# Weight conversion in a gated recurrence with an activation layer: three VectorE operations a tile instead of six, listed beside the first two groups' chunks

## The chip, the cores and the metric

One core of one Trainium2 chip. The metric is the device time of one launch in microseconds (us); the time before is the median of three runs. The engines are named as the profile names them: PE (TensorE, with its weight loads as PEld), DVE (VectorE), ACT (ScalarE), POOL (GpSimd) and SP (SyncE, here the engine that issues nearly all transfers).

## The reference

Inputs are q, k, v, a_re and a_im of shape (4, 8, 768, 48) and two weight matrices, w_in (384 x 2048) and w_out (2048 x 384), which are float64; the output is float32, 3072 x 384.

```
mag = sqrt(a_re^2 + a_im^2);  scale = min(mag, 0.999) / (mag + 1e-6)
a = (a_re + i a_im) * scale
for t in range(768):                       # for each of 4 x 8 heads
    S = a[t][:, None] * S + outer(k[t], v[t])     # S is complex, 48 x 48
    y[t] = q[t] @ real(S)
x = y as (4*768) x (8*48)
h = x @ w_in;  g = h * cos(h);  out = g @ w_out
```

## The kernel before

The 768 steps of each of four sequences are cut into chunks of 128 steps; two chunks make a group (G = 2), so there are 24 chunks and 12 groups. The recurrence is computed in chunks: decays are turned into logarithms and phases and summed along the steps by matmuls with a triangular matrix (L666, L703); scaled and turned keys and queries are transposed; a chunk's scores and values are matmuls; a state passes from chunk to chunk.

For each group the work comes in stages, each a function:

- g_log, g_prod, g_angle (L631 to L697): logarithms, exponentials and the arctangent on ACT, with DVE and POOL operations between, in scratch tiles that exist once. g_prod also sends a row through DRAM and back by six small transfers (L679).
- gates (L840): g_phase (L699), g_trig (L712), g_stack (L720), then four f_transpose (L733; for both chunks the keys kT and the queries qT). An f_transpose is one DVE block transpose (L738) and twelve small transfers issued by SP (L747).
- chunks (L851): f_scores (L752), f_state (L782) and f_out (L763) for the two chunks, then f_xt (L801), ten transfers that assemble the columns for the layer.
- mm1 (L812), eight times a group: the first layer's matmuls for 256 columns of the hidden dimension (L817), then x cos(x) by ACT (L823, L623) and DVE (L824, L826, L828).
- mm2 (L831), twice a group: the second layer's 16 matmuls (L834), a copy out of PSUM by ACT (L837) and the output's transfer.

The main loop (L873) is a software pipeline: turn `it` does the gates of group it, the chunks of group it-1, mm1 of group it-2 and mm2 of group it-3. In a turn mm2 is listed first; the others are woven: weave (L863) gives every step of a part a place between the part's two bounds and lists all steps in the order of their places. The list is a priority and not the order itself: the framework lets each engine take the earliest listed instruction that its timing model finds ready, and fixes each engine's order so; each engine then executes its instructions strictly in that order.

The weights arrive as float64 and have to become float32. weight_parts (L564) cuts them into 28 tiles, 12 of w_in (128 x 512) and 16 of w_out (128 x 384). from_double (L578) loads a tile of 64-bit words by a transfer from SP (L586, two buffers `raw`), and works on the high and low 32-bit words, which are every second word of `raw`. DVE moves exponent and mantissa into place (L591), adds the sign (L593), adds the three top bits of the low word (L595), and takes the rounding bit (L597); POOL adds it as an integer (L599); DVE takes the exponent (L601) and sets to zero what is too small for float32 (L603). These are six DVE operations and one POOL operation a tile, with two buffers `t` for the rounding bit and the exponent.

All 28 tiles are listed in turn 0, in the last four fifths of group 0's gates (L884).

When the fast path has ended, a flag decides whether the general path has to run: the tile `least` collects whether a decay became too small; its minimum goes through DRAM onto one partition and into a register (L906 to L919).

Of the kernel before, what the change touches and what calls it, by code (L numbers as in the profile page):

```python
# [485 lines left out]
def fast_path(ctx, tc, q, k, v, a_re, a_im, moe_w_in, moe_w_out, out, least):  # L486
# [91 lines left out]
    def from_double(dst, src):  # L578

        n = dst.shape[1]
        raw = stage.tile([C, n], I64, tag="raw", name="raw")
        nc.sync.dma_start(out=raw, in_=src)  # L586
# [4 lines left out]
        nc.vector.tensor_scalar(out=bits, in0=hi, scalar1=3, scalar2=0x3FFFFFF8,  # L591
                                op0=ALU.logical_shift_left, op1=ALU.bitwise_and)
        nc.vector.scalar_tensor_tensor(out=bits, in0=hi, scalar=0xC0000000, in1=bits,  # L593
                                       op0=ALU.bitwise_and, op1=ALU.bitwise_or)
        nc.vector.scalar_tensor_tensor(out=bits, in0=lo, scalar=29, in1=bits,  # L595
                                       op0=ALU.logical_shift_right, op1=ALU.bitwise_or)
        nc.vector.tensor_scalar(out=t, in0=lo, scalar1=28, scalar2=1,  # L597
                                op0=ALU.logical_shift_right, op1=ALU.bitwise_and)
        nc.gpsimd.tensor_tensor(out=bits, in0=bits, in1=t, op=ALU.add)  # L599
        e = stage.tile([C, n], U32, tag="t", name="t")  # L600
        nc.vector.tensor_scalar(out=e, in0=hi, scalar1=20, scalar2=0x7FF,  # L601
                                op0=ALU.logical_shift_right, op1=ALU.bitwise_and)
        nc.vector.scalar_tensor_tensor(out=dst, in0=e, scalar=897.0, in1=dst,  # L603
                                       op0=ALU.is_ge, op1=ALU.mult)


# [205 lines left out]
    def mm1(g, jp):  # L812
# [10 lines left out]
        nc.scalar.activation(out=turn, in_=ps, func=AF.Identity, scale=INV_TWO_PI, bias=quarter_b)  # L823
# [7 lines left out]
    def mm2(g, i):  # L831
        ps = pm.tile([C, DM], F32, tag="m", name="op")
        for j in range(NJ):
            nc.tensor.matmul(ps, lhsT=X[g]["gate"][j // 2][:, j % 2, ts(i, C)], rhs=w_out[:, j],  # L834
                             start=(j == 0), stop=(j == NJ - 1))
# [36 lines left out]
    weights = weight_parts()  # L872
    for it in range(NG + 3):  # L873
# [22 lines left out]
def kernel(ctx, tc, q, k, v, a_re, a_im, moe_w_in, moe_w_out, out):  # L896
# [7 lines left out]
    fast_path(tc, q, k, v, a_re, a_im, moe_w_in, moe_w_out, out, least)  # L904
# [4 lines left out]
    line_d = scratch.tile([D2], F32, name="line_d")  # L909
    nc.sync.dma_start(out=line_d, in_=low.rearrange("p o -> (p o)"))  # L910
    line = keep.tile([1, D2], F32, name="line")
# [39 lines left out]
```

## Time and profile before

| | us |
|---|---|
| median of 3 runs (844.55 to 846.62) | 845.02 |
| the profiled execution, whole | 846.44 |
| its span, first to last instruction | 844.6 |
| PE busy (81% of the span) | 682.8 |
| DVE busy (62%) | 526.6 |
| PEld busy (60%) | 506.9 |
| ACT busy (40%) | 338.8 |
| POOL busy (18%) | 152.3 |

A row of a group has the line, the engine, the operation, out<-in by the names of the program, the shapes and the count, then the busy time of the group in us and the mean of one in ns, then the idle time of the engine just before these instructions and what ended it. A row of a timeline has the start and the duration in us. A row of the waits has the waiting instruction, what it waited for, the sum in us, the count and the longest. In the page's strips each of the 40 digits is the busy share of one slice in tenths.

### The profile page before, as it was taken

How to read it: one execution, taken by the hardware profiler on the slowest of the kernel's cores; microseconds unless marked ns; L12 is line 12 of the kernel's file. 1: busy time of each engine (PE TensorE's matmuls, PEld its weight loads, DVE VectorE, ACT ScalarE, POOL GpSimd, SP SyncE). 2: the span in 40 equal slices, each digit the busy share in tenths (PEclk: the TensorE clock that was granted, in tenths of full speed). 3: DMA queues.
4: the chain of work that ended last, by engine and by line, in shares of the span. 5: the costliest groups of instructions: out<-in, count | busy, mean ns of one | idle time of the engine just before them, and what ended most of it. 6: DMA issues, size and time to landing. Idle time of an engine off the chain costs nothing.

```text
span 844.6 us, 10236 instructions
## 1 busy us (share of the span) xinstructions
PE 682.8 (81%) x3464; PEld 506.9 (60%) x3464; DVE 526.6 (62%) x833; ACT 338.8 (40%) x492; POOL 152.3 (18%) x96
## 2 busy tenths in 40 slices
PE   1201043368999999999999999999999999999997
PEld 0000023256678587586785875867858758678684
DVE  3997988666468566485675764856757648335060
ACT  5313001415535645356345453563454534214140
POOL 1433433320120300301203003012030030000000
PEclk9999975579999999999999999999999999999999
DMA  8533347225243362352622623526226231210000
GB/s 181 124 118 102 99 138 167 53 60 98 51 96 73 67 127 51 62 115 51 125 49 54 119 49 62 116 51 131 45 54 117 50 70 29 51 45 15 24 0 22
DMA packets 251335, 65.66 MB, mean 78 GB/s; under 512 B 230270, under 2 KB 247678, under 8 KB 251274
## 3 DMA queue, kind: packets, MB, share of 16 engines
q1 hardware_dynamic: 250674, 64.62, 36.0%
q8 instruction: 29, 0.48, 0.2%
q10 hardware_dynamic: 600, 0.30, 0.1%
q14 instruction: 32, 0.26, 0.1%
HBM read 36.51 MB, written 4.76 MB: 49 GB/s over the span
## 4 chain that ended last, share of the span: by engine, by line
PE 56%; DVE 15%; SPq 9%; ACT 8%; POOL 6%; issue 3%; DMA 3%; DVEq 0%; POOLq 0%; ACTq 0%
PE hp L817 23%; PE op L834 18%; SPq L747 7%; PE sc L758 4%; PE sp L789 2%; POOL m L650 2%; PE yp L772 2%; POOL w_out L599 2%; PE lgs L666 2%; ACT rs L623 2%; PE phs L703 2%; PE yp L776 2%; PE phs L706 1%; DVE gate L826 1%; ACT L622 1%
## 5 line engine op out<-in xcount | busy, mean ns | idle before, releaser
L817 PE MATMUL hp<-xT,w_in 128*128 128x256 f32 x1152 | 267.5, 385 | 4.3 <-DVE gate L828 3.7
L834 PE MATMUL op<-w_out,gate 128*128 128x384 f32 x768 | 251.1, 486 | 0.0
L817 PEld LDWEIGHTS hp<-xT,w_in 128*128 128x128 f32 x1152 | 214.8, 192 | 36.8 <-DVE gate L828 4.1
L834 PEld LDWEIGHTS op<-w_out,gate 128*128 128x128 f32 x768 | 145.9, 190 | 99.2
L823 ACT ACTIVATE turn<-hp,quarter_b 128x512 f32<-128x512 f32 x96 | 65.8, 685 | 111.2 <-PE hp L817 110.0
L623 ACT ACTIVATE gate<-gate 128x512 f32<-128x512 f32 x96 | 60.1, 627 | 91.6 <-DVE gate L826 89.8
L828 DVE TENSOR_TENSOR gate<-hp,gate 128x512 f32<-128x512 f32 x96 | 65.4, 685 | 37.1 <-ACT gate L623 35.2
L824 DVE TENSOR_SCALAR gate<-turn 128x512 f32<-128x512 f32 x96 | 40.3, 420 | 75.7 <-ACT turn L823 74.5
L666 PE MATMUL lgs<-m,sums 128*128 128x384 f32 x48 | 22.8, 606 | 73.2 <-POOL m L650 73.2
L826 DVE TENSOR_TENSOR gate<-turn,gate 128x512 f32<-128x512 f32 x96 | 65.5, 685 | 1.7
L795 POOL TENSOR_TENSOR state<-state,end 96x384 f32<-96x384 f32 x16 | 16.4, 1023 | 263.1 <-DVE state L793 166.7
L758 PEld LDWEIGHTS sc<-qT,kT 96*128 96x128 f32 x384 | 51.7, 201 | 16.4 <-issue 10.4
L666 PEld LDWEIGHTS lgs<-m,sums 128*128 128x128 f32 x48 | 9.6, 222 | 84.5 <-POOL m L650 80.3
L837 ACT COPY ot<-op 128x384 f32<-128x384 f32 x24 | 11.3, 472 | 121.0 <-PE op L834 113.8
L758 PE MATMUL sc<-qT,kT 96*128 96x128 f32 x384 | 52.4, 286 | 8.2 <-DMA qT<-tr 8.2
L650 POOL TENSOR_TENSOR m<-m,rs 128x768 f32<-128x768 f32 x12 | 21.7, 1809 | 206.4 <-ACT rs L623 204.1
L703 PE MATMUL phs<-sq,sums 128*128 128x384 f32 x48 | 22.4, 556 | 43.5 <-DVE sq L694 43.5
L772 PE MATMUL yp<-atm,v 128*48 128x128 f32 x384 | 39.4, 289 | 21.2 <-DVE atm L760 21.2
L760 DVE TENSOR_TENSOR atm<-sc,causal 128x512 f32<-128x512 f32 x48 | 32.7, 682 | 20.6 <-PE sc L758 20.6
L708 DVE TENSOR_SCALAR ph<-phs 128x384 f32<-128x384 f32 x24 | 13.3, 554 | 50.4 <-PE phs L706 36.3
L772 PEld LDWEIGHTS yp<-atm,v 128*48 128x48 f32 x384 | 23.0, 128 | 30.2 <-issue 24.9
L653 DVE SCALAR_TENSOR_TENSOR sq<-mag,sq 128x768 f32<-128x768 f32 x12 | 11.5, 959 | 46.8 <-POOL mag L652 46.8
(72 smaller groups left out, 824.4 us busy)
## 6 DMA issues: line engine op xcount, KB each, us to landing
kT<-tr SPq DMA_DIRECT2D x288, 32.0 KB, 2.0
qT<-tr SPq DMA_DIRECT2D x288, 32.0 KB, 1.8
raw<-in_moe_w_in_dram SPq DMA_DIRECT2D x12, 512.0 KB, 4.0
raw<-in_moe_w_out_dram SPq DMA_DIRECT2D x16, 384.0 KB, 3.4
re<-in_a_re_dram SPq DMA_DIRECT2D x24, 192.0 KB, 3.2
im<-in_a_im_dram SPq DMA_DIRECT2D x24, 192.0 KB, 4.2
k<-in_k_dram SPq DMA_DIRECT2D x24, 192.0 KB, 3.9
q<-in_q_dram SPq DMA_DIRECT2D x24, 192.0 KB, 3.9
```

What stands on the lines that cost most here:

```text
L623: chain(nc.scalar.activation(func=func, **kw))
L666: nc.tensor.matmul(ps, lhsT=sums, rhs=x["lg"][:, ts(i, DM)], start=True, stop=True)
L703: nc.tensor.matmul(ps, lhsT=sums, rhs=x["turn"][:, ts(i, DM)], start=True, stop=first)
L747: nc.sync.dma_start(out=place[ts(b, 32), a], in_=tr[ts(a, 32), b])
L758: nc.tensor.matmul(ps[:, h], lhsT=y["kT"][:, hh * HH + h], rhs=queries(y, hh * HH + h), start=True, stop=True)
L772: nc.tensor.matmul(ps[ds(side * 64, D), p], lhsT=vals[:, 2 * p + side], rhs=y["atm"][:, 2 * p + side], start=True, stop=(state is None))
L817: nc.tensor.matmul(ps[:, ji], lhsT=w_in[:, dc, ts(jp * 2 + ji, C)], rhs=x["xT"][:, dc].rearrange("p g t -> p (g t)"), start=(dc == 0), sto ...
L823: nc.scalar.activation(out=turn, in_=ps, func=AF.Identity, scale=INV_TWO_PI, bias=quarter_b)
L824: nc.vector.tensor_scalar(out=cs, in0=turn, scalar1=ROUND, scalar2=ROUND, op0=ALU.add, op1=ALU.subtract)
L826: nc.vector.tensor_tensor(out=cs, in0=turn, in1=cs, op=ALU.subtract)
L828: nc.vector.tensor_tensor(out=gate, in0=ps, in1=cs, op=ALU.mult)
L834: nc.tensor.matmul(ps, lhsT=X[g]["gate"][j // 2][:, j % 2, ts(i, C)], rhs=w_out[:, j], start=(j == 0), stop=(j == NJ - 1))
```

## The change

from_double now has three DVE operations a tile. The high word is moved and given its sign as before. The low word goes through an ACT Identity: read as an integer, multiplied by 2^-29, plus 2^23, written as an integer; so it is rounded to the bits that float32 keeps and carries a one in the exponent. POOL adds that to the high part. A result is thereby twice the weight, which is taken back by the scale at L823 and by a multiplication in place of the copy at L837. Nothing is set to zero any more. Instead DVE takes the exponent by two shifts into a single buffer `e`, and an ACT Relu of 897 minus the exponent, written over `e`, adds up along the tile into one column of a new tile `odd`; any value above zero sets the flag for the general path. This check needs a reduction, a comparison and one more small transfer at the end.

The 12 tiles of w_in are now listed in turn 1, over the whole turn beside the gates of group 1 and the chunks of group 0, and the 16 tiles of w_out in turn 2, beside the gates of group 2, the chunks of group 1 and mm1 of group 0. Turn 0 has no weights and is woven like all others.

```diff
-        t = stage.tile([C, n], U32, tag="t", name="t")
+        low = stage.tile([C, n], U32, tag="low", name="low")
+        e = stage.tile([C, n], U32, tag="e", name="e", bufs=1)
         bits = dst.bitcast(U32)
         nc.vector.tensor_scalar(out=bits, in0=hi, scalar1=3, scalar2=0x3FFFFFF8,
                                 op0=ALU.logical_shift_left, op1=ALU.bitwise_and)
         nc.vector.scalar_tensor_tensor(out=bits, in0=hi, scalar=0xC0000000, in1=bits,
                                        op0=ALU.bitwise_and, op1=ALU.bitwise_or)
-        nc.vector.scalar_tensor_tensor(out=bits, in0=lo, scalar=29, in1=bits,
-                                       op0=ALU.logical_shift_right, op1=ALU.bitwise_or)
-        nc.vector.tensor_scalar(out=t, in0=lo, scalar1=28, scalar2=1,
-                                op0=ALU.logical_shift_right, op1=ALU.bitwise_and)
-        nc.gpsimd.tensor_tensor(out=bits, in0=bits, in1=t, op=ALU.add)
-        e = stage.tile([C, n], U32, tag="t", name="t")
-        nc.vector.tensor_scalar(out=e, in0=hi, scalar1=20, scalar2=0x7FF,
-                                op0=ALU.logical_shift_right, op1=ALU.bitwise_and)
-        nc.vector.scalar_tensor_tensor(out=dst, in0=e, scalar=897.0, in1=dst,
-                                       op0=ALU.is_ge, op1=ALU.mult)
+        nc.scalar.activation(out=low, in_=lo, func=AF.Identity, scale=2.0 ** -29, bias=carrier_b)
+        nc.gpsimd.tensor_tensor(out=bits, in0=bits, in1=low, op=ALU.add)
+        nc.vector.tensor_scalar(out=e, in0=hi, scalar1=1, scalar2=21,
+                                op0=ALU.logical_shift_left, op1=ALU.logical_shift_right)
+        nc.scalar.activation(out=e.bitcast(F32), in_=e, func=AF.Relu, scale=-1.0, bias=least_e_b,
+                             accum_out=odd[:, ds(next(odds), 1)])
...
-        nc.scalar.activation(out=turn, in_=ps, func=AF.Identity, scale=INV_TWO_PI, bias=quarter_b)
+        nc.scalar.activation(out=turn, in_=ps, func=AF.Identity, scale=INV_TWO_PI / in_scale,
+                             bias=quarter_b)
...
-        nc.scalar.copy(out=ot, in_=ps)
+        nc.scalar.mul(out=ot, in_=ps, mul=1.0 / (in_scale * out_scale))
...
-    weights = weight_parts()
+    parts = weight_parts()
+    weights = {1: parts[:-NJ], 2: parts[-NJ:]}
...
-        if it == 0:
-            weave((gates(0), 0.0, 1.0), (weights, 0.2, 1.0))
-            continue
         if 0 <= o < NG:
             for i in range(G):
                 mm2(o, i)
         weave((gates(g) if g < NG else (), 0.0, 0.5),
               (chunks(c) if 0 <= c < NG else (), 0.0, 1.0),
+              (weights.get(it, ()), 0.0, 1.0),
...
+    even = keep.tile([C, 1], F32, name="even")
+    nc.vector.tensor_reduce(out=even, in_=odd, axis=AX.X, op=ALU.max)
+    nc.vector.tensor_scalar(out=even, in0=even, scalar1=0.0, scalar2=None, op0=ALU.is_le)
...
+    line_d = scratch.tile([D2 + C], F32, name="line_d")
+    nc.sync.dma_start(out=line_d[0:D2], in_=low.rearrange("p o -> (p o)"))
+    nc.sync.dma_start(out=line_d[D2:D2 + C], in_=even.rearrange("p o -> (p o)"))
```

More of the change, by code (lines that the diff above doesn't have):

```diff
@@ L485, in fast_path @@
 @with_exitstack
-def fast_path(ctx, tc, q, k, v, a_re, a_im, moe_w_in, moe_w_out, out, least):
+def fast_path(ctx, tc, q, k, v, a_re, a_im, moe_w_in, moe_w_out, out, least, odd):
     nc = tc.nc
@@ L903 @@
     least = keep.tile([D2, 2 * H], F32, name="least")
[L904 removed]
+    C = 128
+    odd = keep.tile([C, moe_w_in.shape[0] // C * 4 + moe_w_out.shape[0] // C], F32, name="odd")
+    fast_path(tc, q, k, v, a_re, a_im, moe_w_in, moe_w_out, out, least, odd)
     low = keep.tile([D2, 1], F32, name="low")
     nc.vector.tensor_reduce(out=low, in_=least, axis=AX.X, op=ALU.min)
+    even = keep.tile([C, 1], F32, name="even")
+    nc.vector.tensor_reduce(out=even, in_=odd, axis=AX.X, op=ALU.max)
+    nc.vector.tensor_scalar(out=even, in0=even, scalar1=0.0, scalar2=None, op0=ALU.is_le)
     scratch = ctx.enter_context(tc.tile_pool(name="scratch", bufs=1,
                                              space=bass.MemoryType.DRAM))
[L909 to L911 removed]
+    line_d = scratch.tile([D2 + C], F32, name="line_d")
+    nc.sync.dma_start(out=line_d[0:D2], in_=low.rearrange("p o -> (p o)"))
+    nc.sync.dma_start(out=line_d[D2:D2 + C], in_=even.rearrange("p o -> (p o)"))
+    line = keep.tile([1, D2 + C], F32, name="line")
     nc.sync.dma_start(out=line, in_=line_d.unsqueeze(0))
```

6 lines of the change are left out of this document (added).

## The prediction

> **What bounds the kernel now.** I read the page first, for the span and for where TensorE is idle, then the stretches, cut at the point that matters, then the groups by shape, and last the timelines of single engines. The page shows two different kernels in one span:
>
> ```profile
> span 844.6 us, 10236 instructions
> ...
> PE   1201043368999999999999999999999999999997
> ...
> DVE  3997988666468566485675764856757648335060
> ACT  5313001415535645356345453563454534214140
> ...
> PEclk9999975579999999999999999999999999999999
> ```
>
> A slice is 21.1 us. From the tenth or eleventh slice on TensorE is full and nothing else is. In the first ten it is mostly idle, and VectorE is the engine with nines. So the time is a lead-in plus a full-TensorE stretch, and the border I choose is the first matmul of the second layer for group 0 (L834), which needs nearly everything that the lead-in makes: the converted weights, two groups of attention, and the first layer of group 0.
>
> ```profile
> 188.97 1.56 PE L817 MATMUL hp<-xT,w_in 128*128 128x256 f32 x6
> ...
> 219.15 8.55 PE L834 MATMUL op<-w_out,gate 128*128 128x384 f32 x26
> ```
>
> The stretches cut there (columns: TensorE, its weight loads, VectorE, ScalarE and GpSimd busy, each with its instructions, then granted clock, DMA share, GB/s):
>
> ```profile
> 0.00:20.00 20.00, 2.92 (x4) 1.17 (x4) 5.32 (x12) 11.18 (x15) 3.77 (x6) 1.00 0.81 184
> 20.00:160.00 140.00, 28.39 (x130) 19.39 (x130) 119.88 (x219) 26.39 (x34) 51.90 (x35) 0.84 0.47 119
> 160.00:219.15 59.15, 42.95 (x236) 34.03 (x237) 35.02 (x52) 22.79 (x34) 9.30 (x6) 0.77 0.37 71
> 219.15:844.60 625.45, 608.53 (x3095) 452.31 (x3093) 366.39 (x553) 278.42 (x411) 87.37 (x49) 1.00 0.33 66
> ```
>
> Behind 219.15 TensorE is busy 608.53 of 625.45 us (97%). Before it, TensorE is busy 74.3 of 219.15 us, and VectorE 119.88 of the 140 us from 20 to 160 (86%). Each us by which L834 starts earlier is a us off the end, as long as the 625.45 us behind it stay as they are. Call the start of L834 T; now T = 219.15.
>
> **VectorE's part of the conversion.** These are all of its groups, 28 tiles, 12 of w_in and 16 of w_out:
>
> ```profile
> L593 DVE SCALAR_TENSOR_TENSOR w_out<-raw,w_out 128x384 uint32<-128x384 uint32 x16 | 10.4, 652 | 0.0
> L595 DVE SCALAR_TENSOR_TENSOR w_in<-raw,w_in 128x512 uint32<-128x512 uint32 x12 | 9.8, 815 | 0.0
> L603 DVE SCALAR_TENSOR_TENSOR w_out<-t,w_out 128x384 f32<-128x384 uint32 x16 | 8.9, 558 | 9.9 <-POOL w_out L599 9.9
> L595 DVE SCALAR_TENSOR_TENSOR w_out<-raw,w_out 128x384 uint32<-128x384 uint32 x16 | 8.8, 551 | 0.0
> L591 DVE TENSOR_SCALAR w_in<-raw 128x512 uint32<-128x512 uint32 x12 | 8.2, 686 | 0.0
> L603 DVE SCALAR_TENSOR_TENSOR w_in<-t,w_in 128x512 f32<-128x512 uint32 x12 | 8.2, 683 | 2.8 <-POOL w_in L599 2.8
> L593 DVE SCALAR_TENSOR_TENSOR w_in<-raw,w_in 128x512 uint32<-128x512 uint32 x12 | 8.2, 681 | 0.0
> L591 DVE TENSOR_SCALAR w_out<-raw 128x384 uint32<-128x384 uint32 x16 | 6.7, 420 | 0.0
> L601 DVE TENSOR_SCALAR t<-raw 128x384 uint32<-128x384 uint32 x16 | 5.7, 353 | 0.0
> L597 DVE TENSOR_SCALAR t<-raw 128x384 uint32<-128x384 uint32 x16 | 5.6, 353 | 0.0
> L601 DVE TENSOR_SCALAR t<-raw 128x512 uint32<-128x512 uint32 x12 | 5.0, 417 | 0.0
> L597 DVE TENSOR_SCALAR t<-raw 128x512 uint32<-128x512 uint32 x12 | 5.0, 416 | 0.0
> ```
>
> Out go L595 (9.8 + 8.8), L597 (5.0 + 5.6) and L603 (8.2 + 8.9): 46.3 us. What stays is L591 (14.9), L593 (18.6) and a TENSOR_SCALAR of L601's shape with two shifts in place of a shift and a mask (10.7): 44.2 us. With L603 goes its wait for GpSimd's sum, 9.9 + 2.8 us on VectorE. VectorE's work ahead of T falls from 5.32 + 119.88 + 35.02 = 160.2 us to 113.9, of which 5.3 lie in the first 20 us, which are spent on the loads and group 0's first chain and do not change. That leaves 108.6 us behind 20.
>
> How fast it can be packed is what I have to choose. From 20 to 160 the profile has it at 0.856, from 20 to 219.15 at 154.9 / 199.15 = 0.778. At the first T = 20 + 108.6 / 0.856 = 147, at the second 20 + 108.6 / 0.778 = 160. With no gap at all it would be 129. The weights' new place in the lists speaks for the better half: their work can now lie beside the chunks and the first layer of group 0, where VectorE has gaps today (35.02 of 59.15 us), and no longer has to be over before group 1's gates. I take the middle, T = 153: 66 us earlier.
>
> **What ScalarE takes over.** Two activations a tile, 56 in all: an Identity with a bias column, and a Relu with a bias column and an accumulator. No row shows them on integers, on every second word, or with an accumulator. The nearest rows:
>
> ```profile
> L623 ACT ACTIVATE gate<-gate 128x512 f32<-128x512 f32 x96 | 60.1, 627 | 91.6 <-DVE gate L826 89.8 <-DVE flag L916 1.8
> ...
> L622 ACT ACT_TABLE_LOAD x24 | 30.8, 1283 | 3.0 <-issue 2.6
> ...
> L691 ACT ACTIVATE rs<-sq,half_b 128x768 f32<-128x768 f32 x12 | 11.2, 936 | 0.4 <-ACT sq L623 0.2
> ...
> L623 ACT ACTIVATE mag<-m 128x768 f32<-128x768 f32 x12 | 10.1, 840 | 19.7 <-DVE qs L728 19.4
> ```
>
> Without a bias column 256 elements more cost 840 - 627 = 213 ns, 0.83 ns each, so an Identity with a column is 936 - 213 = 723 ns at 512 and 936 - 320 = 616 ns at 384. Both activations: 12 x 1.446 + 16 x 1.232 = 37 us. Bounds: without the column's price 12 x 2 x 0.627 + 16 x 2 x 0.520 = 32 us; with every one at the 768-wide 0.936, which leaves 0.2 to 0.3 us for an accumulator, 52 us. ScalarE is busy 11.18 + 26.39 + 22.79 = 60.4 us ahead of T now, so 97 (92 to 113). In 153 us that is 64%. I cost it at nothing on the path; the cover is ScalarE's idle time, and what it costs when that is too small is the first rival below. The Relu needs no table of its own in this sum; if each tile brought a reload, 28 x 1.283 would be 36 us more on ScalarE, inside the first rival below with the dear end passed.
>
> The Trainium skill ("ScalarE: Activation LUTs", Rules for kernel authors) says the opposite of this edit: relu, add and mul belong on VectorE and not on ScalarE. By the same page's figure (What ACT_TABLE_LOAD costs: about 280 ns and 0.833 ns an element with one column operand) the 56 would come to an estimated 36 us, and the sum would not move. Whether the rule holds here is decided by which engine has room; the rows say VectorE has none in the lead-in, and the case in which the rule is right is the first rival.
>
> **GpSimd, the queue of transfers, the listing.** GpSimd keeps its 28 sums (L599), with fewer two-input VectorE operations beside them; nothing is booked for that. SyncE's queue is next to late, so it gets a sum of its own. A group's transposes fill it without a gap, from the first to the last of four such sets:
>
> ```profile
> 204.48 7.94 SPq L747 DMA_DIRECT2D kT<-tr x12
> ...
> 228.09 7.53 SPq L747 DMA_DIRECT2D qT<-tr x12
> ```
> ```profile
> 63.87 0.97 DVE L738 STREAM_TRANSPOSE tr<-ks 128x768 f32<-128x768 f32 x1
> ```
> ```profile
> L586 SPq DMA_DIRECT2D raw<-in_moe_w_out_dram x16: 328/334/352, 84.4 to 144.4; - x16
> L586 SPq DMA_DIRECT2D raw<-in_moe_w_in_dram x12: 327/340/702, 11.9 to 73.6; - x12
> ```
> ```profile
> SPq L586 <- DVE t L601: 25.7, 8, 5.2
> SPq L586 <- DVE w_in L591: 19.1, 4, 6.9
> SPq L586 <- DVE w_out L595: 18.3, 10, 3.2
> ```
>
> That is 31.1 us a group, and two groups' must pass before T. Group 0's first transpose is at 63.87 now, behind five tiles' worth of conversion since 37; without most of these I estimate 44. So 44 + 62 + 28 x 0.34 for the weights' issues + about 8 for the ten issues that assemble group 0's columns (counted at the transposes' 0.65) + about 10 for the rest of chunk 1 and the first layer gives T = 134 if the queue never stands. Today it stands 25.7 + 19.1 + 18.3 = 63.1 us for a free weight buffer, and then everything queued behind such a load stands too: k and q of a group, its transposes, its columns. If all 63.1 stayed, T = 197. Fewer VectorE operations hold a buffer now, but a ScalarE one does as well; the moved loads stand among group 1's and group 2's transposes. I take 10 to 20 us of it, 144 to 154, which agrees with the 153.
>
> The added end (a second reduction, a comparison, one more small transfer) is on the chain of the flag; it needs only the gates of the last group and the weights, while TensorE still has two layers to do. Cost: nothing. The changed scale at L823 and the multiplication instead of the copy at L837 are one instruction for one.
>
> **The sum.** 219.15 to 153 is -66. The profiled execution took 846.4 us with 844.6 from first to last instruction: 846.4 - 66 = 780.4. The median of the three runs, 845.0, lies 1.4 under it, so I forecast 779.
>
> **Rivals.** (1) ScalarE becomes the bound. Over 50 us it is never busier than this:
>
> ```profile
> 300.00:350.00 50.00, 48.93 (x264) 37.42 (x263) 35.94 (x55) 27.65 (x40) 7.37 (x5) 1.00 0.42 83
> ```
>
> 0.553. At that share 97 us take T = 176, 802 us; the dear end, 113 us, takes T = 204, 830. For it: ScalarE works in order, and its special functions are a chain. Against it: ScalarE's idle time there is spent on waiting for VectorE, which gets shorter. Chance 0.17.
>
> (2) The listing does nothing, because the queues' order isn't the list's. For it:
>
> ```profile
> 37.23 0.95 DVE L639 TENSOR_TENSOR m<-m,sq 128x768 f32<-128x768 f32 x1
> ...
> 40.64 0.95 DVE L728 TENSOR_TENSOR ks<-Q,rs 128x768 f32<-128x768 f32 x1
> ```
>
> L639 is group 1's and is listed behind all weights and all of group 0's gates, yet it runs before group 0's L728. Then only the 46.3 us count, at 0.856: -54, T = 165, 791. Against it: w_out is converted before group 1's gates go on today, as listed. Chance 0.12.
>
> (3) Slower: ScalarE's queue holds VectorE. The buffer of the exponents (e) is single, so VectorE's shift for tile k+1 waits for ScalarE's Relu of tile k; if that stands behind an activation that waits for PSUM, a transfer or a table, VectorE stands, in order, with group 1's chain behind it, which ScalarE itself waits for. The measure is ScalarE's share ahead of T: with 97 us it breaks even at 97 / 219 = 0.44. From 160 to 219.15 it is 22.79 / 59.15 = 0.385 now; at that T = 253 and the time 879. Against it: such a ring needs the wait at nearly every tile, and a Relu takes 0.7 us. Chance 0.05.
>
> (4) It isn't taken as meant: an exponent under the bound sets the flag and the general path runs behind the fast one. Even its two layers alone repeat TensorE's 608.53 us in great part; over 1200. These weights are normal with a spread of 1/20, far from such an exponent. Chance 0.01.
>
> (5) Better: VectorE packed without gaps, T = 129, 755, and under it only if the border isn't the right one. Chance 0.07.
>
> **How the numbers follow.** The forecast itself (T from 144 to 170) has 0.58. The low end is case 5's 755. The high end, 820, takes in the middle of (1) and most of the way to its dear end and to the 823 of a queue that stands as long as today; left out are (3), (4), a part of (1) and the least of (5), about 0.15. A measurement of this kernel (844.55 to 846.62) can tell about 0.3%. Faster by more than that: all but (3) and (4), less 0.01 for a case (3) near its break-even: 0.93. Same: 0.01. Slower: 0.06.
>
> **What would show it.** Right: L834 first starts between 144 and 165; VectorE's busy time ahead of it is near 114 us and its share 0.8 or more; ScalarE's near 97; behind it 620 to 630 us, with TensorE at 97%; group 0's first transpose near 44; the queue's waits for a weight buffer fall to under 20 us. Wrong: L834 waits for w_out's last tiles; the new activations take over 0.94 us or bring table loads; VectorE waits for ScalarE's Relu; the stretch behind L834 grows, which would mean that the border moved work instead of shortening it.

## The result and the profile after

The changed kernel takes 824.6 us (median of 4 runs, 823.37 to 826.59) against 845.82 us for the kernel before on the same chip (844.55 to 847.43): a ratio of 0.975, 95% interval 0.9723 to 0.9778. It is about 21 us faster, and I had forecast 66 (779, range 755 to 820). Below, differences between kernels are differences of such ratios times 845 us, since each ratio was taken on one chip; an interval is about 0.003 on each side, so 3 us, and a difference of two is sure to about 4.

The page's first lines and four strips:

```profile
span 823.1 us, 10293 instructions
...
PE   1217286766899999999999989999999999999997
...
DVE  2876454957685574864954856757658458234060
ACT  5552615663666345453571562464545624123140
...
PEclk9956576897999999999999999999999999999999
```

Before, VectorE had nines in slices 2, 3 and 5. One is left, in slice 8; from slice 2 on it is now 4 to 8 tenths busy in the others ahead of TensorE's full stretch. TensorE does more in the first ten slices, and yet it becomes full only in the twelfth, where it was full in the eleventh: it started earlier, but ran with gaps for longer.

The stretches, cut at the first matmul of the second layer for group 0 (L841, which was L834), and then the same stretches cut once more at the second group's first L841 (247.64 after, 274.74 before):

```profile
0.00:20.00 20.00, 2.93 (x4) 1.17 (x4) 4.97 (x15) 10.76 (x15) 3.77 (x6) 1.00 1.07 184
20.00:160.00 140.00, 69.07 (x337) 52.92 (x338) 92.77 (x135) 66.66 (x105) 41.84 (x27) 0.69 0.48 106
160.00:168.85 8.85, 7.66 (x31) 5.95 (x30) 7.40 (x14) 5.11 (x10) 2.10 (x2) 0.91 0.49 111
168.85:823.10 654.25, 617.45 (x3095) 454.81 (x3094) 383.52 (x593) 293.87 (x447) 98.92 (x61) 0.98 0.35 71
168.85:247.64 78.79, 61.04 (x284) 41.96 (x283) 54.13 (x95) 43.42 (x77) 21.00 (x17) 0.91 0.50 114
247.64:823.10 575.46, 556.41 (x2813) 412.85 (x2811) 329.39 (x499) 250.45 (x370) 77.91 (x44) 0.99 0.33 65
```

The kernel before:

```profile
219.15:274.74 55.59, 54.01 (x283) 40.41 (x282) 36.92 (x55) 28.14 (x42) 8.67 (x5) 1.00 0.38 76
274.74:844.60 569.86, 554.52 (x2813) 411.91 (x2811) 329.46 (x498) 250.29 (x370) 78.70 (x44) 1.00 0.32 65
```

T came 50.3 us earlier (219.15 to 168.85). The stretch behind it grew from 625.45 to 654.25, so 28.8 us were given back: 23.2 between the first and the second group's second layer (78.79 against 55.59) and 5.6 later. What is left is 21.5 us of span. Of the 23.2, 16.2 are TensorE standing idle (78.79 - 61.04 = 17.75 us against 55.59 - 54.01 = 1.58). The other 7.0 are longer busy time for nearly the same matmuls (284 against 283), at a granted clock of 0.91 against 1.00; what lowered the clock there was not tested. The idle part is visible in TensorE's timeline, where idle time and its releaser stand in brackets:

```profile
168.85 3.39 PE L841 MATMUL op<-w_out,gate 128*128 128x384 f32 x10
173.31 3.49 PE L841 MATMUL op<-w_out,gate 128*128 128x384 f32 x10 [1.07 <-POOL w_out L600]
181.83 1.49 PE L841 MATMUL op<-w_out,gate 128*128 128x384 f32 x2 [5.02 <-POOL w_out L600]
...
194.24 2.93 PE L841 MATMUL op<-w_out,gate 128*128 128x384 f32 x4 [7.55 <-POOL w_out L600]
...
227.56 1.56 PE L841 MATMUL op<-w_out,gate 128*128 128x384 f32 x4 [1.90 <-POOL w_out L600]
```

The second layer of group 0 starts at 168.85 and then stands tile by tile on w_out, whose last tile comes at 227.56. Before, its first 26 matmuls ran in one piece of 8.55 us. The releaser named is GpSimd's sum, but GpSimd itself waits for its inputs; one has to ask when the raw tiles arrive. SyncE's queue answers (stretches of it, with the transposes of group 1 from 79.86 and of group 2 from 152.85):

```profile
98.68 7.83 SPq L753 DMA_DIRECT2D kT<-tr  x12
106.55 0.60 SPq L589 DMA_DIRECT2D raw<-in_moe_w_in_dram  x1
107.25 7.52 SPq L753 DMA_DIRECT2D qT<-tr  x12
...
122.20 2.35 SPq L814 DMA_DIRECT2D xT<-yT  x3
```
```profile
163.43 0.53 SPq L589 DMA_DIRECT2D raw<-in_moe_w_out_dram  x1
164.06 7.56 SPq L753 DMA_DIRECT2D qT<-tr  x12
171.73 0.52 SPq L589 DMA_DIRECT2D raw<-in_moe_w_out_dram  x1
172.35 7.82 SPq L753 DMA_DIRECT2D kT<-tr  x12
180.29 0.53 SPq L589 DMA_DIRECT2D raw<-in_moe_w_out_dram  x1
180.93 12.53 SPq L753 DMA_DIRECT2D qT<-tr  x12
193.57 0.52 SPq L589 DMA_DIRECT2D raw<-in_moe_w_out_dram  x1
```

One load of weights, then 12 transfers of a transpose, then one load. Only four of the 28 loads are issued ahead of 40 us, and the fifth is the one at 106.55. And the columns that assemble group 0's input (L814) come at 122, behind all of group 1's transposes, so the first layer of group 0 starts its matmuls at 128.51.

### The profile page after: what moved, and what is told of

Same layout as the page of the kernel before. It is cut to its first block, busy times and chain, and to the rows that moved or that the text cites. A ratio compares the mean times of both kernels' runs of the same rounds, so it can differ in the third digit from the quotient of the medians.

```text
span 823.1 us, 10293 instructions
## 1 busy us (share of the span) xinstructions
PE 697.1 (85%) x3464; PEld 514.9 (63%) x3464; DVE 488.7 (59%) x754; ACT 376.4 (46%) x576; POOL 146.6 (18%) x96
## 4 chain that ended last, share of the span: by engine, by line
PE 53%; SPq 15%; DVE 12%; ACT 9%; issue 4%; DMA 3%; POOL 3%; DVEq 0%; ACTq 0%; POOLq 0%
PE hp L823 20%; PE op L841 18%; SPq L753 12%; PE sc L764 3%; ACT rs L629 2%; PE lgs L672 2%; POOL m L656 2%; PE phs L709 2%; PE yp L778 2%; PE sp L795 2%; DVE gate L833 2%; PE phs L712 1%; PE yp L782 1%; ACT L628 1%; SPq L545 1%
## 5 line engine op out<-in xcount | busy, mean ns | idle before, releaser
L823 PE MATMUL hp<-xT,w_in 128*128 128x256 f32 x1152 | 272.9, 390 | 16.0 <-DMA xT<-yT 8.6
L841 PE MATMUL op<-w_out,gate 128*128 128x384 f32 x768 | 256.3, 490 | 17.3 <-POOL w_out L600 17.1
L823 PEld LDWEIGHTS hp<-xT,w_in 128*128 128x128 f32 x1152 | 218.4, 194 | 53.1 <-DVE gate L835 8.7
L841 PEld LDWEIGHTS op<-w_out,gate 128*128 128x128 f32 x768 | 145.8, 191 | 118.5 <-POOL w_out L600 21.3
L672 PE MATMUL lgs<-m,sums 128*128 128x384 f32 x48 | 25.1, 657 | 52.2 <-POOL m L656 52.2
L833 DVE TENSOR_TENSOR gate<-turn,gate 128x512 f32<-128x512 f32 x96 | 67.2, 702 | 1.7
L844 ACT ACTIVATE ot<-op 128x384 f32<-128x384 f32 x24 | 11.6, 484 | 114.4 <-PE op L841 114.4
L766 DVE TENSOR_TENSOR atm<-sc,causal 128x512 f32<-128x512 f32 x48 | 32.6, 682 | 18.8 <-PE sc L764 18.6
L729 POOL TENSOR_TENSOR Q<-k,Q 128x768 f32<-128x768 f32 x12 | 25.6, 2130 | 55.8 <-ACT rs L697 19.7
```

The costliest lines, as they stand in the source:

```text
L672: nc.tensor.matmul(ps, lhsT=sums, rhs=x["lg"][:, ts(i, DM)], start=True, stop=True)
L823: nc.tensor.matmul(ps[:, ji], lhsT=w_in[:, dc, ts(jp * 2 + ji, C)], rhs=x["xT"][:, dc].rearrange("p g t -> p (g t)"), start=(dc == 0), sto ...
L833: nc.vector.tensor_tensor(out=cs, in0=turn, in1=cs, op=ALU.subtract)
```

## The experiments

Two theories stood at the start. **V**: VectorE's work in the lead-in sets T, as I had forecast, only sized wrongly. **Q**: the place of the transfers in SyncE's in-order queue sets when weights and columns arrive, and VectorE is not the bound any more. The recorded expectations call the first form of Q **P** (place) and set it against **S**: ScalarE's activations make the conversion slow wherever it is listed, through the single buffer `e`. In edits, "SP" is nc.sync (SyncE's queue) and "ACT" nc.scalar (ScalarE's queue).

**The two halves of the change apart.** new_ops_old_list has the changed conversion at the old place in the lists; old_ops_new_list the old conversion at the new place.

```diff
-    weights = {1: parts[:-NJ], 2: parts[-NJ:]}
+    weights = {}
...
+        if it == 0:
+            weave((gates(0), 0.0, 1.0), (parts, 0.2, 1.0))
+            continue
```

> The changed conversion (three VectorE operations, two activations a tile) with the listing of before: all 28 tiles in turn 0. Theory P (place): in the changed kernel the second layer of group 0 starts at 169 but stands on w_out until 229, because 24 of the 28 weight loads stand in SyncE's queue behind the transposes of groups 1 and 2 (first such load at 106.6, last at 219.9); the halving is worth more than was measured. P expects here all weight loads issued ahead of group 1's transposes, no wait of L841 for w_out, the first L841 near 165 and its last before 192, total 790 to 800. Theory S (ScalarE's part makes the conversion slow, wherever it is listed, by the ring over the single buffer e): the conversion takes as long as before, total 820 to 845.

> The conversion of before (six VectorE operations, none on ScalarE) with the new listing (w_in in turn 1, w_out in turn 2). Theory P: the loads stand as late in SyncE's queue as in the changed kernel, so the second layer of group 0 again waits for w_out, and VectorE has 46 us more; total 825 to 845, so most of what the change gained is the listing's or the halving's only in part. Theory S: without the ring the conversion flows as the loads come, total 815 or less, under the changed kernel.

Measured: 827.3 us, ratio 0.9773 (0.9737 to 0.9809), and 840.18 us, ratio 0.9938 (0.9916 to 0.9960). At the old place the halved operations are worth 19 us, at the new place 16. The new place is worth 5 us with the old operations and 2, less than the interval, with the new ones. The first second-layer matmul of new_ops_old_list starts at 195.94 and never stands on w_out; that of old_ops_new_list starts at 186.95 and stands on it until about 248. So the listing brought T forward by 27 us (195.94 to 168.85) and gave nearly all of it back behind T. The first run missed P: 790 to 800 and a first L841 near 165 were expected, and the time lies in S's 820 to 845. The second lies in P's range. The place of the loads in the queue alone therefore does not explain what the old place costs; S is answered by loads_from_ACT and two_e_buffers below.

**No conversion at all.** The weights' tiles are filled by one transfer each and nothing is computed. This bounds what any cheaper conversion can bring.

```diff
+        flat_q = q.rearrange("b h s d -> (b h s d)")[0:C * dst.shape[1]]
+        nc.sync.dma_start(out=dst, in_=flat_q.rearrange("(p x) -> p x", p=C))
+        return
```

> The changed kernel without any conversion: each of the 28 weight tiles is filled with part of q by one SyncE transfer (half the bytes of a weight tile), so raw, the three VectorE operations, the two activations and GpSimd's sum are left out and the output is not that of the weights. It is the floor of every saving on the conversion. Theory V (the prediction's: VectorE's work ahead of the second layer sets its start): with VectorE's 48 us gone too, the first L841 falls to about 115 to 125 and the total to 745 to 760. Theory Q (SyncE's queue sets it: two groups' transposes, then the columns of group 0, then all of the first layer of group 0): the first L841 stays between 155 and 170, its stretch shrinks to about 24 us, total 785 to 800.

Measured: 792.06 us, ratio 0.9367 (0.9346 to 0.9388). With VectorE's, ScalarE's and GpSimd's part of the conversion gone altogether the kernel still takes 792: the forecast of 779 lay below what the conversion could give. Even here the second layer of group 0 has gaps, and now they end on the plain transfer itself:

```profile
147.79 5.97 PE L844 MATMUL op<-w_out,gate 128*128 128x384 f32 x18
154.89 2.20 PE L844 MATMUL op<-w_out,gate 128*128 128x384 f32 x6 [1.13 <-DMA w_out<-in_q_dram]
...
163.56 2.93 PE L844 MATMUL op<-w_out,gate 128*128 128x384 f32 x4 [3.93 <-DMA w_out<-in_q_dram]
```

Those transfers stand in SyncE's queue among group 2's transposes, at 143.93, 152.21, 160.78 and so on. V cannot make such gaps; Q does. The time lies in Q's range, but the first L844, at 147.79, lies in neither (115 to 125 for V, 155 to 170 for Q).

**The loads out of SyncE's queue.**

```diff
-        nc.sync.dma_start(out=raw, in_=src)
+        nc.scalar.dma_start(out=raw, in_=src)
```

> The changed kernel with the 28 weight loads issued from ScalarE's queue instead of SyncE's; listing and conversion as changed. Theory P: nothing holds the loads behind transposes, w_in is converted before 100 and w_out before 170, L841 does not wait for w_out; about 28 x 0.45 = 13 us of issuing on ScalarE is the price; total 785 to 805. Theory S: ScalarE is the slow link and gets 13 us more work, total 825 or more.

Measured: 803.17 us, ratio 0.9495 (0.9466 to 0.9524), 21.5 us faster than the changed kernel by one word:

```profile
168.79 8.55 PE L841 MATMUL op<-w_out,gate 128*128 128x384 f32 x26
...
179.79 12.42 PE L841 MATMUL op<-w_out,gate 128*128 128x384 f32 x38
...
223.86 8.55 PE L841 MATMUL op<-w_out,gate 128*128 128x384 f32 x26
```

T is where it was (168.79), but the second layer runs through, and the second group's follows 55.07 us later, as before the change (55.59), not 78.79. That is Q: the conversion does the same work on the same engines. It also speaks against S, which expected 825 or more, since ScalarE has the issuing of 28 loads on top.

**A turn earlier, on either queue.** The other way to get loads ahead of the transposes is to list w_in in turn 0 and w_out in turn 1; the second kernel has this and the loads on ACT.

```diff
-    weights = {1: parts[:-NJ], 2: parts[-NJ:]}
+    weights = {0: parts[:-NJ], 1: parts[-NJ:]}
```

> The changed kernel with w_in listed in turn 0 and w_out in turn 1 instead of 1 and 2. Theory P: the last w_out load is issued at about 165 instead of 220, the first L841 comes at 150 to 170 and its stretch lasts about 25 to 35 us instead of 60; total 785 to 805. Theory S: the conversion is as slow, only begun earlier; L841 still waits for GpSimd's sum by tens of us, total over 815.

> The kernel with the weight loads on ScalarE's queue, listed one turn earlier (w_in in turn 0, w_out in turn 1). Theory Q: w_out is no longer late in that kernel, so the earlier listing brings nothing and puts more conversion in front of group 1's chain: within 5 us of 803, or slower by up to 10. Theory P in its simple form (the earlier the tiles, the better): 790 to 798.

Measured: 815.96 us, ratio 0.9644 (0.9609 to 0.9679), and 803.45 us, ratio 0.9498 (0.9471 to 0.9525). On SyncE's queue the earlier turn is 9 us better than the changed kernel; T is later (186.70 against 168.85), and yet the time is shorter, since the second layer of group 0 no longer stands on w_out behind T. P's 785 to 805, with T at 150 to 170, was missed all the same; 815.96 lies just inside S's "over 815", but the waits of L841 that S expected are gone. With the loads on ACT the turn makes no difference, as Q expected. Both runs speak against taking T alone as the measure.

**What the two halves are worth with the loads on ACT.** These two runs ask what VectorE's part really is.

> The operations of before (seven VectorE passes and one GpSimd sum a tile) at the changed listing, raw loads issued from ScalarE's queue: loads_from_ACT (803.2 us) without the halving. If the queue masked VectorE's work, the halving is worth about 40 us here against 16 with the loads on SyncE: 835 to 850, the first second-layer matmul waiting for VectorE's last pass on w_out until 230 or later. If VectorE's work is not on the path: 815 to 822. If the loads on ScalarE's queue now hold ScalarE's own activations (it has no conversion work that paces them): over 850.

> The changed operations at the old listing (all tiles in the first turn, woven with the gates of group 0), raw loads from ScalarE's queue. If the new listing's gain is only that tiles lie where the engines have room, the old listing with a free queue converts ahead of group 0's chain and delays it: 808 to 825, later than 803. If the listing is worth nothing once the loads have a queue of their own: 800 to 806.

Measured: 824.28 us, ratio 0.9763 (0.9747 to 0.9779), and 823.7 us, ratio 0.9753 (0.9736 to 0.9769). The four pairs, each as ratio to the kernel before:

| | loads on SP | loads on ACT |
|---|---|---|
| old operations, old place | 1 | not run |
| old operations, new place | 0.9938 | 0.9763 |
| new operations, old place | 0.9773 | 0.9753 |
| new operations, new place (the change, and its loads on ACT) | 0.975 | 0.9495 |

With the queue freed, the new place is worth 22 us where it was worth 2 with the loads on SP: the listing's gain was real, and SyncE's queue took it. At the old place freeing the queue is worth 2 us only: there all loads are issued ahead of group 1's transposes anyway (in new_ops_old_list the last two from 119.65, the transposes from 125.25). The halving is worth 23 us in place of 16; my expectation of about 40 for a masked VectorE was not met, and 824.28 lies just above the 815 to 822 of its rival. (The expectation above speaks of seven VectorE passes; there are six.) VectorE is again close to full with the old operations:

```profile
20.00:160.00 140.00, 56.83 (x299) 41.48 (x299) 125.27 (x195) 37.63 (x50) 54.24 (x34) 0.83 0.47 112
```

125.27 of 140 us is 0.895, the densest VectorE of all these kernels. Still, taking half of its conversion away brings only 23 us, and these are not VectorE's alone. In ScalarE's timeline of the same run:

```profile
131.47 27.95 ACTq L586 DMA_DIRECT2D raw<-in_moe_w_out_dram  x7
159.69 1.78 ACT L780 COPY yT<-yp 48x512 f32<-48x512 f32 x3 [33.30 <-DMA end<-row]
```

Seven loads, 0.33 us each to issue where nothing holds them, take 27.95 us on ScalarE's queue, and ScalarE's own copies follow only behind them, after 33.3 us of idle time. (The row names a transfer of SyncE as the last releaser; the issues of ScalarE's own queue end at 159.42.) That the loads stand there for a raw buffer, which the six passes hold for longer, is likely and was not tested. What VectorE's work is worth by itself at the new place therefore stays open; 23 us is what halving it brought together with this.

The old place costs 22 us on ACT. There all 28 conversions run ahead of group 1's chain (the last GpSimd sum starts at 99.7). The first transposes of group 1, in old_list_loads_from_ACT and then in loads_from_ACT:

```profile
132.02 7.84 SPq L753 DMA_DIRECT2D kT<-tr  x12
```
```profile
88.89 8.00 SPq L753 DMA_DIRECT2D kT<-tr  x12
```

**The floor with the queue freed.** No conversion, and its plain loads on ACT.

> No conversion at all (the weights' tiles are filled from q by one transfer each, so the second layer's numbers are others), and these 28 transfers are issued from ScalarE's queue. It is the floor of any cheaper conversion with SyncE's queue freed of the loads. If the place of the loads in SyncE's queue costs time even when nothing is converted: the first piece of the second layer starts near 148 and does not stand, and the time is 775 to 785 against 792. If what is left of the lead-in is the chain of gates, transposes and columns: 789 to 793.

Measured: 787.69 us, ratio 0.9323 (0.9296 to 0.9350). That is 4 us under the floor on SP, and between the two expectations: the queue costs a little even there, and most of what is left is other work. T is 160.55, and behind it:

```profile
160.55:785.60 625.05, 608.28 (x3095) 452.37 (x3093) 365.50 (x552) 278.76 (x411) 87.21 (x49) 1.00 0.34 66
```

625.05 us, the 625.45 of the kernel before almost to the digit. Without a conversion left beside or behind T, the border was a sound one. What remains ahead of it here, 160.55 us, is work other than the conversion: loads, gates, transposes, columns and the first layer of the first groups. It is no floor for T: no_conversion with its loads on SP starts the second layer at 147.79, and columns_from_ACT below, with the whole conversion, at 153.95.

**The columns and the transposes.** columns_from_ACT adds the column transfers of groups 0 and 1 to loads_from_ACT; the next two move half of the transposes' transfers of groups 0 to 2 (a % 2, with g < 3), alone and on top of columns_from_ACT.

```diff
+                eng = nc.scalar if g < 2 else nc.sync
-                nc.sync.dma_start(out=xt[ds(row % C, n), row // C],
+                eng.dma_start(out=xt[ds(row % C, n), row // C],
```
```diff
+                eng = nc.scalar if g < 3 and a % 2 else nc.sync
-                nc.sync.dma_start(out=place[ts(b, 32), a], in_=tr[ts(a, 32), b])
+                eng.dma_start(out=place[ts(b, 32), a], in_=tr[ts(a, 32), b])
```

> The kernel with the weight loads on ScalarE's queue, and besides the ten transfers that assemble the columns (L814) of groups 0 and 1 also issued from ScalarE. Theory Q: the columns of group 0 no longer stand behind group 1's transposes (they were issued from 127.5 to 136), so the first layer of group 0 starts 20 to 30 us earlier; the first L841, 168.8 without this, comes at 140 to 155, the total 775 to 793. Theory V: VectorE's work is the same, so the first L841 and the total stay within 4 us of 168.8 and 803.

> The changed kernel with half of the 48 transpose transfers of groups 0, 1 and 2 issued from ScalarE's queue instead of SyncE's; weight loads and columns stay in SyncE's queue. If the length of SyncE's queue (31 us of transposes a group) is what holds the lead-in: the transposes of groups 1 and 2 take 16 to 20 us instead of 35 to 41, the weight loads behind them come 15 us (w_in) to 30 us (w_out) earlier, the second layer of group 0 no longer stands on w_out until 229, and the time falls from 824.6 to 795 to 810. If the engines' chains hold it (VectorE's and ScalarE's work on the next group's gates), the transfers are issued sooner but wait for the same tiles: over 818.

> The kernel with weight loads and the columns of groups 0 and 1 on ScalarE's queue (800.4 us), and in addition half of the transpose transfers of groups 0, 1 and 2. If the queue still holds it there: the second group's second layer comes 15 us or so earlier than 222, the time is 780 to 790, below the 792 of the kernel without conversion and loads on SyncE. If what is left is the chain of gates, phases and transposes' own data of groups 2 and 3 on VectorE and ScalarE: 797 to 801. If ScalarE's own issuing (0.6 us for each of 24 transfers a group, in line with its activations) costs more than SyncE's relief: over 803.

Measured: 800.39 us, ratio 0.9451 (0.9427 to 0.9475); 818.3 us, ratio 0.9692 (0.9664 to 0.9721); 837.63 us, ratio 0.9903 (0.9877 to 0.9929). The columns alone bring the first layer of group 0 forward by 39 us (from 134.03 in loads_from_ACT) and T by 15:

```profile
95.00 2.04 PE L824 MATMUL hp<-xT,w_in 128*128 128x256 f32 x4 [4.00 <-DMA xT<-yT]
...
153.95 6.29 PE L842 MATMUL op<-w_out,gate 128*128 128x384 f32 x19
```

The time hardly follows (about 4 us), since the second group's second layer starts at 222.34 in place of 223.86. That group's own transposes come no earlier (their issues end at 123.86, in loads_from_ACT at 122.87); what else holds it was not followed. So T fell into Q's 140 to 155, while the time missed Q's 775 to 793 and lies within V's 4 us of 803.

Half of the transposes on ACT give 5 us, less than the 15 to 30 expected; 818.3 lies just above the 818 of the other outcome. On top of the loads and the columns they cost 38 us, the third outcome (over 803). ScalarE's timeline of that run shows what that outcome named, its own issuing:

```profile
45.34 4.36 ACTq L754 DMA_DIRECT2D kT<-tr  x6
...
57.83 3.77 ACTq L754 DMA_DIRECT2D qT<-tr  x6
61.66 0.93 ACT L629 ACTIVATE m<-m,tiny_b 128x768 f32<-128x768 f32 x1 [18.76 <-DMA qT<-tr]
```

The 24 issues of group 0 run from 45.34 to 61.60 nearly without a gap, so 16 of the 18.8 us for which ScalarE stands are the issuing of the transfers, and 2.5 are a wait ahead of the first. In group 1 it stands for 17.2 us, 16.1 of them issuing (96.96 to 113.05). But half_transposes_from_ACT has the same two stretches (18.64 and 17.07 us) and is 5 us faster than the changed kernel, so they alone are not the 38 us; what makes them so dear when loads and columns are on ScalarE's queue as well stays open.

**The buffers.** The ring of the third rival, alone and in the best version; and a third raw buffer (low then single, to fit).

```diff
-        e = stage.tile([C, n], U32, tag="e", name="e", bufs=1)
+        e = stage.tile([C, n], U32, tag="e", name="e", bufs=2)
```
```diff
-        raw = stage.tile([C, n], I64, tag="raw", name="raw")
+        raw = stage.tile([C, n], I64, tag="raw", name="raw", bufs=3)
...
-        low = stage.tile([C, n], U32, tag="low", name="low")
+        low = stage.tile([C, n], U32, tag="low", name="low", bufs=1)
```

> The changed kernel with two buffers for the exponents instead of one, so that VectorE's shift of the next tile need not wait for ScalarE's Relu. The prediction's third rival (ScalarE holds VectorE through this ring): faster than the changed kernel by 10 us or more, under 815. Theories P and Q (place in the queue): within 3 us of 824.6.

> Weight loads and the columns of groups 0 and 1 on ScalarE's queue (800.4 us), and two buffers for the exponents instead of one. The ring over e gave 3.4 us in the changed kernel. If VectorE and ScalarE wait for each other there: 795 to 798. If what is left is the chain of group 2's gates and transposes: 799 to 802.

> The changed kernel with three buffers for the raw weights in place of two (one for the low words in place of two, so that they fit). If the wait of loads for a free buffer, about 22 us of SyncE's time, is on the path: 805 to 812. If the loads are late because of what stands ahead of them in the queue: 821 to 826.

Measured: 821.23 us, ratio 0.9700 (0.9677 to 0.9723); 800.3 us, ratio 0.9481 (0.9455 to 0.9507), not better than with one; 827.79 us, ratio 0.9790 (0.9756 to 0.9823), no gain, and just above the 821 to 826 expected. The ring is worth 4 us in the changed kernel and nothing in the best version. The third raw buffer prices no free buffer by itself: the low words have one buffer less, and SyncE's waits at the loads stay at 22 to 23 us. The loads of w_out still stand between group 2's transposes there (163.16, 171.42, 179.98). What shows that their place makes them late is loads_from_ACT, which has the two buffers of the changed kernel.

The best version that was run is columns_from_ACT, 800.39 us; against the changed kernel that is 3% less for two edits of a queue.

## Why the prediction was wrong

**The direction was right, the size wrong by a factor of three.** Two steps failed, and one term of a sum. Of the 45 us that were missing (66 forecast, 21.5 of span measured), 16 lie ahead of T (153 forecast, 168.85 measured) and 29 behind it.

**Failed: "Each us by which L834 starts earlier is a us off the end, as long as the 625.45 us behind it stay as they are."** They became 654.25. The border needed "the converted weights", I wrote; but its first matmul needs only the first tile of w_out, and with w_out listed in turn 2 the other 15 could come later, which they did, until 227.56. I had named the sign of it ("L834 waits for w_out's last tiles", "moved work instead of shortening it") and given it no chance of its own. A step that the change itself moves past the border cannot be priced by the border. one_turn_earlier and loads_from_ACT show both sides: T 18 us later and 9 us faster, T the same and 21.5 us faster. A border one group later would have held: from the second group's first second-layer matmul to the end of the span it is 569.9 us in the kernel before, 575.5 in the changed one, and 569.8 to 580.3 in all the runs here.

**Failed: VectorE's packing as the measure of T.** I divided 108.6 us of VectorE work by 0.78 to 0.856. Ahead of the new T it was busy 4.97 + 92.77 + 7.40 = 105.1 us, less than the 113.9 forecast only because 12 of w_out's 16 tiles were converted behind T, at 100.2 / 148.85 = 0.67 behind the first 20. It was waiting, not packed, and its longest wait up to T was for the weights' loads:

```profile
DVE w_in L595 <- DMA raw<-in_moe_w_in_dram: 16.1, 5, 5.5
```

Across the runs with the loads on ACT and the new place, the halving brings 23 us for 90.5 - 47.7 = 42.8 us of VectorE's work (before's rows against after's), and taking the rest away, with ScalarE's and GpSimd's share, 14.5 us (0.9495 to 0.9323) for 47.7: 0.5 and 0.3 us for each (the first with ScalarE's standing in it), where I had taken 66 us for 46.3 and a better packing, more than one for one. The high share of VectorE before was a fact; that its work was worth its whole length was not. With no conversion at all T is still 147.79 with the loads on SP and 160.55 with them on ACT, so the other work of the lead-in holds T there by itself; which step of it does was not taken apart.

**The queue's sum had the right idea and a wrong last term.** Group 0's first transpose came at 40.85 on VectorE (forecast 44), and SyncE's four largest waits at the loads (L589) came to 12.1 + 5.7 + 2.6 + 1.0 = 21.4 us (I took 10 to 20). But "about 10 for the rest of chunk 1 and the first layer" was 168.85 - 128.51 = 40 from the first layer's start alone: its matmuls wait for the last columns (3.92 us at 135.33), and after that for its gates, which go through VectorE and ScalarE tile by tile (2.11 us at 146.99, 3.47 at 157.59). And the sum added the loads as 28 times 0.34 us, as if it made no difference where they stand; it counted the queue's length, not which load is behind which transposes. That is what the 21.5 us of loads_from_ACT are, all of them behind T.

**The terms that were only sized.** VectorE's three operations take 47.7 us against 44.2:

```profile
L601 DVE TENSOR_SCALAR e<-raw 128x512 uint32<-128x512 uint32 x12 | 9.4, 782 | 0.0
L597 DVE SCALAR_TENSOR_TENSOR w_in<-raw,w_in 128x512 uint32<-128x512 uint32 x12 | 9.1, 762 | 0.0
...
L597 DVE SCALAR_TENSOR_TENSOR w_out<-raw,w_out 128x384 uint32<-128x384 uint32 x16 | 9.0, 562 | 0.0
...
L601 DVE TENSOR_SCALAR e<-raw 128x384 uint32<-128x384 uint32 x16 | 8.0, 500 | 0.0
```

L597 (L593 before) became shorter on w_out (652 to 562 ns) and longer on w_in (681 to 762), and the second TENSOR_SCALAR longer on both (353 to 500, 417 to 782). In sum L601 is 6.7 us above its 10.7, and L595 and L597 together 3.2 us below their 33.5. ScalarE's share is 43.0 us against 37, inside its 32 to 52; no table was loaded for it:

```profile
L599 ACT ACTIVATE low<-raw,carrier_b 128x384 uint32<-128x384 uint32 x16 | 10.3, 641 | 9.0 <-DMA raw<-in_moe_w_out_dram 6.3 <-POOL w_out L600 2.7
...
L603 ACT ACTIVATE e<-e,least_e_b 128x384 f32<-128x384 uint32 x16 | 9.8, 612 | 12.6 <-DVE e L601 12.6
...
L599 ACT ACTIVATE low<-raw,carrier_b 128x512 uint32<-128x512 uint32 x12 | 9.1, 762 | 23.3 <-DMA raw<-in_moe_w_in_dram 12.5 <-DMA qT<-tr 9.5 <-POOL w_in L600 1.2
...
L603 ACT ACTIVATE e<-e,least_e_b 128x512 f32<-128x512 uint32 x12 | 8.6, 719 | 9.7 <-DVE e L601 9.6
...
L603 ACT ACTIVATION_READ_ACCUMULATOR e<-e,least_e_b 128x1 f32 x28 | 5.2, 187 | 0.0
```

**The rivals.** (1) ScalarE as the bound: the time fell inside its range (802 to 830), for another reason. ScalarE is busy 82.5 us ahead of T, 0.49 of it, below the 0.553 that it reaches elsewhere; its idle time ahead of the new activations ends on transfers and on VectorE, as the rows above show; and loads_from_ACT gives it more to do and is 21.5 us faster. The rule of the Trainium skill that the prediction named ("ScalarE: Activation LUTs", Rules for kernel authors: relu, add and mul belong on VectorE) is not borne out in this place: the edit that moved such work to ScalarE was worth 16 to 23 us in the three pairs above. (2) "The listing does nothing" was right about the listing's worth, 2 us with the new operations, but not about its mechanism (nor its 791): the order did follow the lists, and SyncE's queue took the gain. (3) The ring: 4 us. (4) did not happen; w_out's spread is in fact 1/45, not 1/20, which changes nothing in it. (5) lay below the floor of 788.

**Open.** Behind the second group's second layer loads_from_ACT takes 580.3 us (804.2 - 223.86), the kernel without conversion 569.8. These 10 us lie in single groups further on and were not followed. Nor was it taken apart which of the steps ahead of T holds it when nothing is converted.

## What to carry to other kernels

A border matmul is a measure only for work that the change leaves in front of it: when work is moved past it, price the last operand that the layer needs, not the first. Before costing an engine's work at its full length, bound the gain by leaving that work out; here the bound was 57 us, below my forecast of 66. And when transfers are relisted, write down for each what stands ahead of it in its in-order queue: the length of the queue can be harmless where the order is not. A second queue is not free either, because its engine works through it in order: 24 issues took 16 us of ScalarE's time, and seven loads that stood there held its own work for 33.

## What was not expected of the hardware

The same load, issued from another engine, was worth 21.5 us. The Trainium skill ("DMA: Bandwidth & Descriptors", Issuing engines are not separate DMA queues) says that issuing from several engines saves only the sequencer's time for it, which is usually small beside the transfer. In this case that time was the cost: the 24 transfers of one chunk's keys and queries took SyncE about 15.8 us to issue (8.29 + 7.53 from 79.86 on, 32 KB a transfer), and a load queued behind them waits for all of it.

Operations of VectorE were held up beside GpSimd. From VectorE's timeline and then GpSimd's, at the same place:

```profile
205.62 2.75 DVE L601 TENSOR_SCALAR e<-raw 128x384 uint32<-128x384 uint32 x1
```
```profile
205.51 0.87 POOL L801 TENSOR_TENSOR state<-state,end 96x384 f32<-96x384 f32 x1 [1.15 <-DVE state L799]
206.34 1.80 POOL L728 TENSOR_TENSOR P<-q,P 128x768 f32<-128x768 f32 x1
```

The operation whose median is 0.35 us lasts 2.75, until GpSimd's second one is over at 208.14. The Trainium skill ("SBUF — State Buffer", SBUF: two separate sides) tells of a pair of ports that GpSimd and VectorE, in its two-port modes or with two inputs from SBUF, lock against each other for a whole instruction; the trace agrees with it. Nine of the 84 conversion operations on VectorE (two of L595, two of L597, five of L601) began while a GpSimd operation ran and lasted 0.2 to 2.4 us longer than the median of their shape, 9.5 us in sum. The two kept lines of the kernel before (L591 and L593) have five such cases with 5.9 us, which the forecast's means already held; the difference, 3.6 us, accounts for the 3.5 above the forecast 44.2. Seven more began beside a GpSimd operation and were not lengthened: four in its last 0.1 us, and three beside one (from 155.47) that itself took 2.33 us where its median is 1.00. An accumulator, for its part, costs a separate instruction of 187 ns on ScalarE.
